# An mLSTM state update: three ScalarE copies and one GpSimd addition in place of three VectorE operations

## The chip, the core and the metric

The kernel runs on one core of one Trainium2 chip, as one launch. The core has five engines that run side by side, each through its own list of instructions, strictly in the order of that list: TensorE (PE, matmuls; PEld is its loading of weights), VectorE (DVE), ScalarE (ACT), GpSimd (POOL) and SyncE (SP, which here starts all DMAs). Where an instruction needs another engine's result it waits on a semaphore, and everything behind it on its own engine waits too. The metric is the device time of the launch in microseconds (us), lower is better. Before the change it is 406.48 us, the median of three runs (405.6 to 406.5).

## What is computed

Three layers one after the other, all in float32. The first is an mLSTM over 2 batches, 8 heads, 768 steps and heads of width 40. The changed line belongs to it:

```
for t in range(S):
    m_new = np.maximum(f_gate[t] + m, i_gate[t])
    f_stab = np.exp(f_gate[t] + m - m_new);  i_stab = np.exp(i_gate[t] - m_new);  m = m_new
    C = f_stab * C + i_stab * outer(v[t], k[t])        # state, 40 x 40 per head
    n = f_stab * n + i_stab * k[t]
    y[t] = sigmoid(o_gate[t]) * (C @ q[t]) / max(|n . q[t]|, 1)
```

The second layer takes x (1536 tokens x 320) to `max(x@w1, x@w2, x@w3) @ w_out` with an inner width of 768. The third takes that to `mish(z @ w_in) @ w_out2` with an inner width of 2048.

## The kernel before, in words

**The mLSTM in chunks.** The 768 steps are cut into six chunks of 128, so with two batches there are 12 units (u = 2 * chunk + batch). Unit u works on 128 steps of all eight heads of one batch at once. Its pieces, with the names that the rows use: `spread` broadcasts the forget gates with eight matmuls into two PSUM banks (fp, L139); `decay` turns each bank into decay factors with a VectorE scan (dt, L124); `scores` multiplies keys and queries into the same two banks (sc, L162), so the scores of a unit can't be written before both of its scans have read them; `decayed` multiplies scores and decays (dt, L167); `passed` and `queries` make the queries scaled by the decay since the chunk's start (cp on PE, cb on VectorE, L178); `values` and `keys` scale v and k on GpSimd (vp L173, kp L184). `numer` (it, L204 and L206) is the sum of two parts: the scaled queries times the state carried in (st), and the decayed scores times vp. `denom` and `gated` turn it into the unit's output (den, sg, xn), `transpose_x` brings that to the layout of the next layer (xp, xh) and `lower_x` makes its low part (xl).

**The state.** There is one tile st per batch, 120 x 8 x 41: three heads stacked on the partitions, a column block of 41 for each head, with zeros wherever a partition's head is not that column's. `outer` (sp, L256) multiplies kp and vp in three matmuls into one PSUM bank; its off-diagonal blocks are to be dropped. `carry` first multiplies st by the chunk's decay (three ScalarE instructions, L268), and then adds the wanted blocks of sp: three VectorE operations (L270), each for every third head, multiply sp by a mask column and add st. Units 2 to 9 do this, eight times in all (units 0 and 1 start the state with L264, units 10 and 11 need no state after them).

**The layers behind.** Float32 values are split into a high and a low part, and one product is eight matmuls of 512 columns (`mm8`, L339). `up(blk, m)` makes three such products (mm_m_0 to mm_m_2) for a block of 512 tokens, takes their maximum (ACT L354, DVE L356 twice) and splits it (ACT hh L358, POOL hl L359). The three products share three PSUM banks, so the product after next waits for the reading of the one before. Their weights arrive as raw bits and are decoded: dec (ACT L285), low (DVE L292, L294), dec (DVE L296), then split (ACT L307 to L309, POOL L310 to L312). There are nine such pieces w_0 to w_8, then three for `down` (wo; L330 to L332), later more for the third layer. Two buffers hold dec, so a piece is started when the split of the piece two before it is done.

**What sets the order.** The first third is written out by hand on all engines, up to unit 3 and the first up(0, 0). The rest is written as plans (PLAN0: `w` load weights, `u` up, `o` load wo, `a` attend, `b` finish of a unit), and a scheduler orders each engine's list from its own model of durations; it sets the lists when the kernel is built, and on the chip they are fixed. Units 0 to 3 are the tokens of block 0, units 4 to 7 those of block 1, and units 8 to 11 those of block 2, so the mLSTM of later units runs between the matmuls of earlier blocks.

Of the kernel before, what the change touches and what calls it, by code (L numbers as in the profile page):

```python
# [8 lines left out]
F32 = mybir.dt.float32  # L9
F32R = mybir.dt.float32r  # L10
AF = mybir.ActivationFunctionType
ALU = mybir.AluOpType
# [3 lines left out]
B, H, S, D = 2, 8, 768, 40  # L16
# [7 lines left out]
VD = D + 1  # L24
# [18 lines left out]
def mlstm_moe_kernel(ctx, tc, fi0, fir, qk2, q3, nat, w13, wo1, wi2, wo2, ident, bmask, out):  # L43
    nc = tc.nc
# [15 lines left out]
    a2 = at.enter_context(tc.tile_pool(name="a2", bufs=2))  # L60
# [12 lines left out]
    bmt = ac.tile([120, H], F32, tag="bmt", name="bmt")  # L73
# [8 lines left out]
    st = [ac.tile([120, H, VD], F32, tag=f"st{b}", name=f"st{b}") for b in range(B)]  # L82
# [177 lines left out]
    def carry(u):  # L260
        c, b = u // B, u % B
        sp = unit[u]["sp"]
        if c == 0:
            return nc.vector.tensor_tensor(st[b], sp[:, 0:H], bmt[:, 0:H].unsqueeze(2).to_broadcast([120, H, VD]), op=ALU.mult)  # L264
        dc = unit[u]["dc"]
        for g in range(3):
            h1 = min(3 * g + 3, H)
            nc.scalar.activation(st[b][:, 3 * g:h1], st[b][:, 3 * g:h1], AF.Copy, scale=dc[:, g])  # L268
        for j in range(3):
            nc.vector.scalar_tensor_tensor(st[b][:, j::3], sp[:, j:H:3], bmt[:, j:j + 1], st[b][:, j::3], op0=ALU.mult, op1=ALU.add)  # L270

    raws = {}

# [117 lines left out]
    with tc.manual_schedule(engines={ET.PE, ET.DVE, ET.SP, ET.Activation, ET.Pool}):  # L391
# [5 lines left out]
        f, i = ft0[:, 0], ft0[:, 1]  # L397
# [69 lines left out]
        nc.scalar.activation(sel40.rearrange("p (r d) -> p r d", d=D), idt[:, P + BH:P + 2 * BH + 1].unsqueeze(2).to_broadcast([P, BH + 1, D]), AF.Copy)  # L467
        denom(0)
        carry(0)
        nc.vector.tensor_tensor_scan(cpr, fr, z1r, 0.0, op0=ALU.mult, op1=ALU.add)  # L470
        nc.scalar.activation(fzr[64:64 + BH], cpr, AF.Copy)
# [13 lines left out]
        nc.scalar.activation(gTr, gq[:, 0:NR * BH], AF.Copy)  # L485
        denom(1)
        carry(1)
        decayed(2, 0)
        decayed(2, 1)
# [52 lines left out]
        fdve = lower_x(3)  # L542
        fpool = load_w13(1)
        carry(2)
        carry(3)
        up(0, 0, 0)
# [221 lines left out]
```

## Time and profile before

| what | before |
|---|---|
| median of 3 runs | 406.48 us (405.6 to 406.5) |
| profiled execution, its own time | 405.76 us |
| its span, first to last instruction | 403.9 us |
| busy share PE / PEld | 97% / 85% |
| busy share DVE / ACT / POOL | 54% / 43% / 39% |
| granted TensorE clock | 1.000 throughout |

The span is what the trace shows, the remaining 1.86 us lie around it. A matmul's end in the trace is modelled, so that two neighbours overlap; the distance between starts tells what one costs in a row of them. Busy shares over the whole span hide stages: up to about 95 us weights are decoded, and DVE, ACT and POOL are busy; behind it PE is busy nearly alone.

### The profile page before, as it was taken

To read this page: it belongs to the slowest core of one execution; us is meant where nothing else is said; L and a number is where in the kernel's file an instruction comes from. 1 tells how busy PE (TensorE), PEld (TensorE's weight loads), DVE (VectorE), ACT (ScalarE), POOL (GpSimd) and SP (SyncE) were. 2 spreads that over 40 slices of the span, in tenths; PEclk is the share of its full clock that TensorE was granted. 3 is DMA by queue.
4 is the path that set the end of the run, shared out by engine and by line. 5 is a ranking of instruction groups with operands and counts; after the bars stand their busy time and mean duration, and the time that the engine had idled before them with its cause. 6 is when DMAs were issued, how large, how long until landed. Compare 5 with 4: busy or idle time off the path is not lost.

```text
span 403.9 us, 6179 instructions
## 1 busy us (share of the span) xinstructions
PE 393.0 (97%) x2380; PEld 345.0 (85%) x2384; DVE 218.1 (54%) x342; ACT 172.4 (43%) x387; POOL 156.6 (39%) x155
## 2 busy tenths in 40 slices
PE   8999999879999999999999999999999999999996
PEld 4977887758898888888888899999898999999996
DVE  7988999998335577305922869972212221222220
ACT  3545655564143212246442586653332333434331
POOL 7556768995313223338851455661000010001000
PEclk9999999999999999999999999999999999999999
DMA  7786455636302011001420234300100000100001
GB/s 202 217 291 190 151 191 197 205 137 185 100 2 82 20 65 68 0 2 43 152 67 0 73 125 137 124 1 2 65 0 2 1 2 0 67 0 2 34 0 34
DMA packets 10410, 32.62 MB, mean 81 GB/s; under 512 B 1405, under 2 KB 4285, under 8 KB 10381
## 3 DMA queue, kind: packets, MB, share of 16 engines
q1 hardware_dynamic: 10381, 32.23, 24.9%
q8 instruction: 19, 0.31, 0.4%
q14 instruction: 10, 0.08, 0.1%
HBM read 30.26 MB, written 1.97 MB: 80 GB/s over the span
## 4 chain that ended last, share of the span: by engine, by line
PE 84%; DVE 8%; POOL 4%; issue 3%; ACT 1%; DVEq 0%; POOLq 0%
PE h L339 22%; PE mm L339 18%; PE o L662 7%; PE o L660 7%; PE o L661 7%; PE it L206 4%; PE mz L370 2%; PE mz L372 2%; PE mz L371 2%; PE fp L139 2%; PE sc L162 2%; DVE dt L124 2%; PE it L204 2%; PE wps L193 2%; PE sp L256 1%
## 5 line engine op out<-in xcount | busy, mean ns | idle before, releaser
L644 DVE TENSOR_TENSOR gl<-g,gh 128x512 fp32r<-128x512 f32 (+1 forms) x64 | 38.3, 599 | 97.3 <-ACT g L643 97.3
L339 PE MATMUL mm<-xh,w 128*128 128x512 f32 x270 | 73.1, 397 | 1.5 <-DVE zraw L356 0.9
L339 PE MATMUL h<-zh,wi 128*128 128x512 f32 (+1 forms) x320 | 67.7, 338 | 0.0
L642 ACT ACTIVATE gh<-h 128x512 fp32r<-128x512 f32 (+1 forms) x64 | 31.4, 491 | 83.6 <-PE h L339 77.6
L339 PEld LDWEIGHTS mm<-xh,w 128*128 128x128 f32 x270 | 49.4, 188 | 12.5 <-DVE zraw L356 1.0
L662 PE MATMUL o<-wo,gl 128*128 128x320 f32 x192 | 59.4, 309 | 0.0
L661 PE MATMUL o<-wo,gh 128*128 128x320 f32 x192 | 59.4, 309 | 0.0
L660 PE MATMUL o<-wo,gh 128*128 128x320 f32 x192 | 59.2, 309 | 0.0
L339 PEld LDWEIGHTS h<-zh,wi 128*128 128x128 f32 x320 | 51.4, 189 | 4.7
L613 POOL TENSOR_TENSOR zl<-zraw,zh 128x512 fp32r<-128x512 f32 (+1 forms) x12 | 13.0, 1091 | 91.5 <-ACT zh L612 91.5
L339 PE MATMUL mm<-xl,w 128*128 128x512 f32 x162 | 46.9, 393 | 0.0
L339 PE MATMUL h<-zl,wi 128*128 128x512 f32 (+1 forms) x192 | 44.5, 338 | 0.0
L359 POOL TENSOR_TENSOR hl<-zraw,hh 128x512 fp32r<-128x512 f32 x18 | 25.9, 1441 | 46.8 <-ACT hh L358 46.7
L356 DVE TENSOR_TENSOR zraw<-zraw,mm 128x512 f32<-128x512 f32 x36 | 24.5, 681 | 29.1 <-PE mm L339 29.0
L660 PEld LDWEIGHTS o<-wo,gh 128*128 128x128 f32 x192 | 36.1, 188 | 1.3
L661 PEld LDWEIGHTS o<-wo,gh 128*128 128x128 f32 x192 | 36.1, 188 | 1.2
L662 PEld LDWEIGHTS o<-wo,gl 128*128 128x128 f32 x192 | 36.1, 188 | 0.0
L339 PEld LDWEIGHTS mm<-xl,w 128*128 128x128 f32 x162 | 30.2, 188 | 6.4
L339 PEld LDWEIGHTS h<-zl,wi 128*128 128x128 f32 x192 | 31.8, 188 | 4.1
L643 ACT ACTIVATE g<-h 128x512 f32<-128x512 f32 (+1 forms) x64 | 31.2, 487 | 0.0
L124 DVE TENSOR_TENSOR_SCAN dt<-fp,idr 128x512 f32<-128x512 f32 x24 | 28.3, 1207 | 2.3 <-PE fp L139 2.2
L206 PE MATMUL it<-vp,dt 128*128 128x41 f32 x192 | 25.0, 271 | 0.0
(138 smaller groups left out, 630.7 us busy)
## 6 DMA issues: line engine op xcount, KB each, us to landing
raw_wo<-in_wo_dram SPq DMA_DIRECT2D x11, 640.0 KB
na<-in_nat_dram SPq DMA_DIRECT2D x12, 484.0 KB
raw_w<-in_w_dram SPq DMA_DIRECT2D x9, 640.0 KB
raw_wi<-in_wi_dram SPq DMA_DIRECT2D x8, 640.0 KB
qall<-in_qk_dram SPq DMA_DIRECT2D x24, 160.0 KB
out_dram<-ob SPq DMA_DIRECT2D x12, 160.0 KB
q<-in_q_dram SPq DMA_DIRECT2D x10, 180.0 KB
idt<-in_ident_dram SPq DMA_DIRECT2D x1, 80.5 KB
```

What stands on the lines that cost most here:

```text
L124: nc.vector.tensor_tensor_scan(dtf[:, j * 512:(j + 1) * 512], unit[u]["fp"][j], idr, 0.0, op0=ALU.mult, op1=ALU.add)
L206: nc.tensor.matmul(it[:, h], t["dt"][:, h], vt[:, h], start=(c == 0), stop=(c == 0 or h == h1 - 1))
L339: nc.tensor.matmul(ps, a, r, start=(k == 0), stop=(k == 7))
L356: tops[blk, m] = nc.vector.tensor_tensor(top, top, pss[i], op=ALU.max)
L359: nc.gpsimd.tensor_tensor(ls, top, h.bitcast(F32), op=ALU.subtract)
L613: nc.gpsimd.tensor_tensor(zl[:, j], zv[:, j], zh[:, j].bitcast(F32), op=ALU.subtract)
L642: mark[blk, m] = nc.scalar.activation(gh, ps, AF.Mish)
L643: nc.scalar.activation(g, ps, AF.Mish)
L644: low[blk, m] = nc.vector.tensor_tensor(gl, g, gh.bitcast(F32), op=ALU.subtract)
L660: nc.tensor.matmul(po, a, whi, start=(m == 0), stop=False)
L661: nc.tensor.matmul(po, a, wlo, start=False, stop=False)
L662: nc.tensor.matmul(po, l, whi, start=False, stop=(m == KF2 - 1))
```

## The change

After the scaling by the decay, the masked product is no longer added by VectorE. ScalarE copies the wanted blocks of sp out of PSUM, times the mask column, into a new SBUF tile nw (three copies, L271 in the new file), and one GpSimd addition adds nw to the whole state tile (L272). The tile nw has one buffer for all units.

```
         for g in range(3):
             h1 = min(3 * g + 3, H)
             nc.scalar.activation(st[b][:, 3 * g:h1], st[b][:, 3 * g:h1], AF.Copy, scale=dc[:, g])
+        nw = a2.tile([120, H, VD], F32, tag="nw", bufs=1, name=f"nw{u}")
         for j in range(3):
-            nc.vector.scalar_tensor_tensor(st[b][:, j::3], sp[:, j:H:3], bmt[:, j:j + 1], st[b][:, j::3], op0=ALU.mult, op1=ALU.add)
+            nc.scalar.activation(nw[:, j::3], sp[:, j:H:3], AF.Copy, scale=bmt[:, j:j + 1])
+        nc.gpsimd.tensor_tensor(st[b], st[b], nw, op=ALU.add)
```

Two lines are added, so from there on the new file's line numbers are higher by two (L285 becomes L287, L339 becomes L341). The scheduler orders the plans anew, and so instructions that the diff doesn't touch stand elsewhere too. Three places follow. In the names the first digits tell the unit, the block or the weight piece (st0 is batch 0, nw2 unit 2, w13_8 the piece w_8, mm0_5_1 the product 5_1 of block 0); the last number only tells tiles apart.

The first is ScalarE's list from the carries of units 2 and 3 on (39 us in the trace of before). Before:

```order
L268 ACTIVATE st0_98<-st0_98,dc2_352 120x123 x2
L268 ACTIVATE st0_98<-st0_98,dc2_352 120x82
L268 ACTIVATE st1_99<-st1_99,dc3_408 120x123 x2
L268 ACTIVATE st1_99<-st1_99,dc3_408 120x82
L285 ACTIVATE dec_w13_2_568<-raw_w13_2_511 128x640
L188 ACTIVATE sg4_626<-na4_583 128x320
L188 ACTIVATE sg5_718<-na5_675 128x320
L154 ACTIVATE dc4_618<-cp4_614 120x3
L354 ACTIVATE zraw_70<-mm0_0_0_533 128x512
```

The same place now:

```order
L268 ACTIVATE st0_98<-st0_98,dc2_352 120x82
L271 ACTIVATE nw2_524<-sp2_475,bmt_88 120x3x41 x2
L271 ACTIVATE nw2_524<-sp2_475,bmt_88 120x2x41
L268 ACTIVATE st1_99<-st1_99,dc3_408 120x123 x2
L268 ACTIVATE st1_99<-st1_99,dc3_408 120x82
L287 ACTIVATE dec_w13_2_572<-raw_w13_2_511 128x640
L188 ACTIVATE sg4_630<-na4_587 128x320
L188 ACTIVATE sg5_722<-na5_679 128x320
L154 ACTIVATE dc4_622<-cp4_618 120x3
L128 ACTIVATE dl4_606<-dt4_603 128x8
L287 ACTIVATE dec_w13_3_632<-raw_w13_3_493 128x640
L154 ACTIVATE dc5_714<-cp5_710 120x3
```

Three copies (nw2) now stand ahead of the decode of w_2, and the reading of the first product (mm0_0_0) has moved behind the decode of w_3 and behind the three copies nw3, which come next in the list.

The second is GpSimd's list at the split of w_8, around the carry of unit 4 (75 to 82 us). Before:

```order
L173 TENSOR_TENSOR vp0_91<-na6_841,gTr_101 128x328
L184 TENSOR_TENSOR kp0_89<-na6_841,dl6_860 128x320
L247 TENSOR_TENSOR xl1_582<-xr4_760,xh1_581 128x3x128
L310 TENSOR_TENSOR w13_8_909<-dec_w13_8_903,w13_8_909 128x512
L311 TENSOR_TENSOR w13_8_909<-dec_w13_8_903,w13_8_909 64x128
L312 TENSOR_TENSOR w13_8_909<-dec_w13_8_903,w13_8_909 64x128
L216 TENSOR_TENSOR sg5_718<-sg5_718,den5_815 128x320
```

And now:

```order
L173 TENSOR_TENSOR vp0_91<-na6_849,gTr_101 128x328
L184 TENSOR_TENSOR kp0_89<-na6_849,dl6_868 128x320
L247 TENSOR_TENSOR xl1_586<-xr4_764,xh1_585 128x3x128
L272 TENSOR_TENSOR st0_98<-st0_98,nw4_774 120x328
L312 TENSOR_TENSOR w13_8_917<-dec_w13_8_911,w13_8_917 128x512
L313 TENSOR_TENSOR w13_8_917<-dec_w13_8_911,w13_8_917 64x128
L314 TENSOR_TENSOR w13_8_917<-dec_w13_8_911,w13_8_917 64x128
L216 TENSOR_TENSOR sg5_722<-sg5_722,den5_821 128x320
```

The addition stands between unit 4's xl and the split of w_8, and the gating of unit 5 (sg5) comes behind both.

The third is TensorE's list from the scores of unit 7 to the numerator of unit 6 (87 to 92 us). Before:

```order
L162 MATMUL sc7_0_937<-qall_93 128x128 x4
L162 MATMUL sc7_1_938<-qall_93 128x128 x4
L150 MATMUL cp7_947<-fzr_97,sel40_96 120x128 x3
L339 MATMUL mm0_4_2_1092<-xh0_103,w13_7_894 128x512 x4
L339 MATMUL mm0_4_2_1092<-xl0_104,w13_7_894 128x512 x3
L339 MATMUL mm0_5_0_1182<-xh0_103,w13_7_894 128x512
L204 MATMUL it6_1018<-st0_98,cb6_881 128x123
```

And now, from the last scores on:

```order
L162 MATMUL sc7_0_945<-qall_93 128x128
L162 MATMUL sc7_1_946<-qall_93 128x128
L341 MATMUL mm0_5_0_1192<-xh0_103,w13_7_902 128x512
L150 MATMUL cp7_955<-fzr_97,sel40_96 120x128 x3
L341 MATMUL mm0_5_0_1192<-xh0_103,w13_7_902 128x512 x3
L341 MATMUL mm0_5_0_1192<-xl0_104,w13_7_902 128x512 x3
L341 MATMUL mm0_5_1_1193<-xh0_103,w13_8_917 128x512 x5
L341 MATMUL mm0_5_1_1193<-xl0_104,w13_8_917 128x512 x3
L204 MATMUL it6_1026<-st0_98,cb6_889 128x123
```

When the numerator of unit 6 is reached, the list of before has one matmul of product 5_0 behind it, and the new one all eight of 5_0 and all eight of 5_1: fifteen matmuls more. The other matmuls ahead of that point (the scores, the spreads and the rest of units 4 to 7) are the same ones.

## Rows read from the trace of the kernel before

**Rows 1.** The page's first part: busy us, share of the span, instructions.

```profile
PE 393.0 (97%) x2380; PEld 345.0 (85%) x2384; DVE 218.1 (54%) x342; ACT 172.4 (43%) x387; POOL 156.6 (39%) x155
```

**Rows 2.** Stretches: length, busy us of each engine, clock, DMA share, GB/s.

```profile
60.00:70.00 10.00, 9.10 (x55) 7.47 (x54) 9.97 (x15) 5.15 (x12) 8.96 (x9) 1.00 0.60 202
70.00:80.00 10.00, 9.27 (x58) 7.61 (x56) 9.01 (x16) 5.92 (x16) 8.85 (x9) 1.00 0.59 188
80.00:90.00 10.00, 6.86 (x44) 5.24 (x43) 9.39 (x13) 6.29 (x13) 9.25 (x9) 1.00 0.45 159
90.00:100.00 10.00, 9.69 (x59) 8.29 (x59) 8.78 (x16) 4.22 (x11) 6.12 (x7) 1.00 0.64 181
100.00:110.00 10.00, 10.00 (x60) 8.15 (x59) 3.29 (x8) 1.68 (x4) 3.68 (x4) 1.00 0.35 107
```

**Rows 3.** PE's groups, 40 to 95 us: busy, mean ns; idle before, releaser.

```profile
L162 PE MATMUL sc<-qall 64*128 64x128 f32 x64 | 8.5, 289 | 3.2 <-DVE dt L124 3.2
```

**Rows 4.** Lines L268 and L270: count, shortest/median/longest ns, first and last start.

```profile
L268 ACT ACTIVATE st<-st,dc x24: 346/384/399, 39.4 to 146.0; 120x123 f32<-120x123 f32 x16, 120x82 f32<-120x82 f32 x8
L270 DVE SCALAR_TENSOR_TENSOR st<-sp,bmt,st x24: 289/330/347, 41.5 to 155.8; 120x123 f32<-120x123 f32 x16, 120x82 f32<-120x82 f32 x8
```

**Rows 5.** Timeline, 39 to 43 us: start, length, engine, line, what, count.

```profile
39.40 1.77 ACT L268 ACTIVATE st<-st,dc 120x123 f32<-120x123 f32 x6
41.08 0.76 ACT L285 ACTIVATE dec_w<-raw_w 128x640 f32<-128x640 f32 x1
41.48 1.50 DVE L270 SCALAR_TENSOR_TENSOR st<-sp,bmt,st 120x123 f32<-120x123 f32 x6
41.61 1.43 POOL L173 TENSOR_TENSOR vp<-na,gTr 128x328 f32<-128x328 f32 x2
42.53 0.57 ACT L354 ACTIVATE zraw<-mm 128x512 f32<-128x512 f32 x1
42.90 0.82 DVE L294 SCALAR_TENSOR_TENSOR low_w<-dec_w,low_w 128x640 int32<-128x640 int32 x1
```

**Rows 6.** Timeline, 55 to 90 us: DVE beside POOL, and carries four and five.

```profile
55.02 0.81 DVE L296 SCALAR_TENSOR_TENSOR dec_w<-raw_w,low_w 128x640 int32<-128x640 int32 x1
72.71 0.80 DVE L270 SCALAR_TENSOR_TENSOR st<-sp,bmt,st 120x123 f32<-120x123 f32 x3
84.14 1.74 DVE L296 SCALAR_TENSOR_TENSOR dec_wo<-raw_wo,low_wo 128x640 int32<-128x640 int32 x1
85.15 1.85 POOL L359 TENSOR_TENSOR hl<-zraw,hh 128x512 fp32r<-128x512 f32 x1
88.89 1.31 POOL L173 TENSOR_TENSOR vp<-na,gTr 128x328 f32<-128x328 f32 x1
89.54 0.80 DVE L270 SCALAR_TENSOR_TENSOR st<-sp,bmt,st 120x123 f32<-120x123 f32 x3
```

**Rows 7.** Timeline, 77 to 83 us: POOL up to unit 5's gating.

```profile
77.06 1.60 POOL L247 TENSOR_TENSOR xl<-xr,xh 128x384 fp32r<-128x384 f32 x1
78.61 1.30 POOL L310 TENSOR_TENSOR w<-dec_w,w 128x512 fp32r<-128x512 f32 x1
81.51 0.85 POOL L216 TENSOR_TENSOR sg<-sg,den 128x320 f32<-128x320 f32 x1
82.40 0.49 DVE L221 TENSOR_TENSOR xn<-it,sg 128x320 f32<-128x320 f32 x1 [0.61 <-POOL sg L216]
```

**Rows 8.** Timeline, 85 to 93 us: PE's waits in brackets, and cb of unit 6.

```profile
87.06 1.16 PE L162 MATMUL sc<-qall 64*128 64x128 f32 x8 [1.39 <-DVE dt L124]
88.58 1.16 PE L162 MATMUL sc<-qall 64*128 64x128 f32 x8 [0.36 <-DVE dt L124]
91.80 0.54 DVE L178 TENSOR_TENSOR cb<-cp,q 120x384 f32<-120x384 f32 x1
92.39 0.48 PE L204 MATMUL it<-st,cb 120*128 120x123 f32 x2 [0.31 <-DVE cb L178]
```

**Rows 9.** The chain that ended last: start, length, what; matmuls behind unit 6's numerator.

```profile
95.96 4.84 PE mm L339 x21
```

## The prediction, written before the changed kernel ran

> **What bounds the kernel now.** I read the busy shares first [rows 1]: PE stands at 97%, the other three at about half. That alone would say that nothing on DVE matters. The stretches say otherwise [rows 2]. From 100 us on PE is full and DVE has a third of its time taken; but in the ten microseconds from 80 on PE is busy for only 6.86, and DVE for 9.39 and POOL for 9.25. The four stretches from 60 to 100 leave PE 0.90 + 0.73 + 3.14 + 0.31 = 5.08 us idle. This is the room that the change can work in; behind it, PE's own list is the time, and what DVE saves there costs and gives nothing. The groups of PE [rows 3] name the largest wait: 3.2 us ahead of the scores, whose two banks have to be read by DVE's scans first. The timeline [rows 8] shows it at work: the scores of unit 7 wait 1.39 and 0.36 us for scans that stand in DVE's queue, and the numerator of unit 6 waits 0.31 us for cb, also on DVE. So up to about 95 us the time is set by a chain that runs through DVE's queue and, at its side, POOL's.
>
> **What is removed.** 24 VectorE operations, 289 to 347 ns each [rows 4], eight groups of three. A group in a row takes 0.80 us [rows 6], so 6.4 us leave DVE in all. Only four groups lie ahead of 95 us: units 2 and 3 (1.50 us together [rows 5]) and units 4 and 5 (0.80 each [rows 6]). The other four lie in stretches where PE is full; they count for nothing.
>
> **What is added on ScalarE.** 24 copies. The trace of before has no such copy of 120 x 3 x 41 out of PSUM. From below, the scalings of the same size follow each other every 1.77 / 6 = 0.295 us [rows 5]; from above, one lasts up to 0.399 us alone [rows 4]. I take the lower, since they stand in a row: 0.89 us for a group, 1.2 at most. ACT is half idle [rows 2], so most of them are covered, with one exception. At the first two carries the list is full: the six scalings start at 39.40, and the decode of w_2 follows at 41.08 [rows 5]. Now three copies stand in front of it, so it ends near 42.73 in place of 41.84. DVE needs that decode for L294, which began at 42.90, when the six removed operations were just done. So DVE, 1.50 us earlier free, waits for ACT, and keeps 0.1 to 0.2 us of it. The six copies also push back the reading of the first product, from 42.53 by roughly 3 to 3.5 us (two groups of 0.89, and the decode and small copies that the new list puts ahead of it). Its bank is wanted again only by the fourth product, and the 16 matmuls of the second and third stand ahead of that, 3.7 us at 0.23 each [rows 9], so this is about covered. I book the first two carries at nothing. Uncovered, it would cost up to 1.8 us, the two groups.
>
> **What is added on GpSimd.** Eight additions of 120 x 328, also not in the trace. The nearest row is vp of 128 x 328: two of them in 1.43 us, 0.72 each [rows 5], and 1.31 us where DVE works beside it [rows 6]. I take 0.75 to 0.9. The first two stand behind two vp that end at 43.04 [rows 5] and ahead of the split of w_2, which has to wait for DVE's decoding of w_2 from 42.90 on in any case; the addition for unit 4 falls where POOL has no room. From xl at 77.06 over the split of w_8 to sg at 81.51 its operations touch each other, and DVE's xn of unit 5 waits 0.61 us for the end of it [rows 7]. The addition goes between, and I count 0.8 us of delay for w_8, for sg and for the decode buffer behind it. The one for unit 5 stands behind xl of that unit near 90 us, ahead of operations that only later matmuls need.
>
> **DVE and POOL against each other.** The final decoding operation lasts 0.81 us at 55.02 and 1.74 at 84.14, where POOL's operation at 85.15 lies beside it [rows 6]; the removed L270 never moves outside 289 to 347 ns [rows 4]. So what is removed is of a kind that was not disturbed, and what is added on POOL may disturb others: by up to 0.93 us each, twice in the full stretch, and not at all if the scans or the readings of products happen to run beside it. I take 0.4 each, the middle. The Trainium skill ("SBUF — State Buffer", section "SBUF: two separate sides") says that a VectorE operation with two SBUF inputs and a GpSimd one take a shared port in turn, whole instructions at a time; the longer row at 84.14 agrees. By it alone each addition could cost DVE its full length, and the full stretch would give up twice 0.75 where I count twice 0.4: 0.7 us more, 403.9 in place of 403.2.
>
> Sum on DVE and POOL up to cb of unit 6: saved 2 x 0.80 = 1.6; lost 0.8 (addition ahead of w_8) + 0.8 (disturbance) + about 0.5 (small waits, an allowance like the 0.61 and 0.31 that rows 7 and 8 show). That is 0.5 us later: cb of unit 6 starts near 92.3 in place of 91.80, and the numerator near 92.9 in place of 92.39 [rows 8].
>
> **What is moved on TensorE, the larger term.** The new list reaches that numerator with fifteen 512-column matmuls more behind it. In the row of 21 that followed the numerator's stretch before, one costs 4.84 / 21 = 0.23 us [rows 9], so 3.45 us of work are taken out of the stretch behind 95 us, which PE bounds, and put into the idle 5.08 us [rows 2]. They have to fit there. Product 5_1 needs w_8, split by 82.3 in my count; 5_0 needs the bank that ACT frees; both are asked for after the scores at about 89. It fits, if the scans come no later than before. Behind the numerator, the cover stays what it was: between the spread of unit 8 and its first scores stand 21 matmuls in either list, 7 + 8 + 6 before, 8 of product 5_2 and 13 of `down` now. So the lead isn't used up by the next wait of the same kind. SyncE's list starts a few loads of later units earlier, one of them ahead of w_8's; the DMA engines are 0.45 to 0.64 busy there [rows 2], and I book nothing for it.
>
> Sum: -3.45 + 0.5 = -2.95 us. Against the profiled execution's own 405.76 this gives 402.8. That execution is at the lower end of the three runs; against the median of 406.48 it gives 403.5. I say 403.2, between the two.
>
> **The rivals.**
>
> *No change: the lead is paid back.* The attention chain, not PE's work, is the clock up to 95 us, and the extra matmuls only stand in front of things that then come later. For it: DVE at 9.97 of 10 and POOL near 9 of 10 from 60 to 70 [rows 2] have no slack, and the additions take POOL's. Against it: the waits of PE [rows 8] are real idle time, and 15 matmuls fill it wherever DVE is. It needs the numerator of unit 6 some 2.3 to 4.6 us later than 92.39: the lost 0.8, the full 1.86 of disturbance and the 1.8 of the first carries uncovered, less 1.6, make 2.9. Time 405.2, within a band of 404.6 to 407.0. The skill's "Perfetto Trace Analysis", section "Optimizing Scalar/DVE Operations", warns that moving work from VectorE to GpSimd may not help; the row at 84.14 speaks for that warning, the low busy shares of the stretch from 100 us on against it.
>
> *Slower: ScalarE's queue holds up the weights.* One buffer holds nw, so the copies for unit 3 wait for the GpSimd addition of unit 2, which waits behind two vp (until 43.04 [rows 5]). Behind these copies stand the reading of the first product and the split of w_2, and then every weight piece in turn, since two decode buffers tie each piece to the one before. If this shift of 1.8 to 2.7 us goes through the chain whole, and the additions cost 1.31 each for units 4 and 5, with 1.86 of disturbance, the numerator comes 1.8 to 2.7 + 2.6 + 1.9 - 1.6 = 4.7 to 5.6 us late, less the 3.45: 1.3 to 2.1 slower, about 407.5. It decides from a numerator that starts later than 97.0 (92.39 + 3.45 + 1.2).
>
> *Faster by more.* POOL's additions hide, no disturbance, and DVE's 1.6 us reach the numerator: -3.45 - 1.6 = -5.05, all the idle there is: 400.7.
>
> **How the numbers follow.** 0.3% of 406.48 is 1.2 us, about what a measurement can tell from no change. Chances: the forecast (with -1.3 to -4.2 around it) 0.50, the faster one 0.12, no change 0.22, slower 0.16. So faster 0.62, same 0.22, slower 0.16. The likeliest case alone gives 402.0 to 405.0. For eight in ten I go from 401.0 up to 407.2: below, about half of the faster case is left out; above, the worse half of the slower one.
>
> **What would show it.** Right: PE's idle time from 60 to 100 us falls from 5.1 us to about 2; unit 6's numerator starts between 91.5 and 94 with product 5_1 done; from there to the end the span is as long as before less 3.45 us; a copy lasts 0.3 to 0.4 us, an addition 0.7 to 0.9; the decode of w_2 on ACT is about 0.9 us later and DVE idles ahead of L294. Wrong: PE waits for a weight split or a product's bank in the first stretch (45 to 60 us); the numerator after 95; new waits for st or for ScalarE behind 100 us; or a scan that comes 2 us later because of the split of w_8.

## The result and the profile after: slower by 0.7%

The changed kernel takes 409.31 us, the median of four runs (408.38 to 409.78), against 406.44 us for the kernel before beside it. The ratio is 1.0073 with an interval of 1.0054 to 1.0093: slower, where 403.2 was forecast. The profiled execution took 408.38 us, the least of the four; its span is 406.5 us.

The page's first part, where [rows 1] stand for before: VectorE gave up 5.2 us, ScalarE took on 6.9 and GpSimd 7.1. TensorE's busy time rose by 1.7 us, although its list holds the same work.

```profile
PE 394.7 (97%) x2384; PEld 345.8 (85%) x2384; DVE 212.9 (52%) x318; ACT 179.3 (44%) x411; POOL 163.7 (40%) x163
```

The stretches that answer to [rows 2], then the ten microseconds around 92 us in pieces of two (columns as in [rows 2]; the clock is the seventh figure, the one before the DMA share).

```profile
60.00:70.00 10.00, 9.50 (x53) 7.37 (x52) 9.97 (x15) 5.86 (x14) 7.44 (x8) 1.00 0.51 176
70.00:80.00 10.00, 9.13 (x59) 7.61 (x59) 8.61 (x14) 6.79 (x18) 8.43 (x8) 1.00 0.51 161
80.00:90.00 10.00, 5.17 (x29) 3.80 (x30) 8.28 (x8) 4.68 (x8) 8.24 (x10) 0.98 0.38 132
90.00:100.00 10.00, 10.00 (x50) 8.50 (x50) 7.03 (x11) 5.95 (x15) 8.35 (x8) 0.68 0.63 213
...
88.00:90.00 2.00, 0.56 (x3) 0.56 (x4) 2.00 (x3) 0.74 (x1) 0.90 (x2) 0.88 0.27 64
90.00:92.00 2.00, 2.00 (x13) 1.77 (x13) 2.00 (x4) 1.46 (x4) 2.00 (x3) 0.50 0.67 264
92.00:94.00 2.00, 2.00 (x8) 1.67 (x8) 1.90 (x3) 1.24 (x6) 2.00 (x2) 0.50 0.00 0
94.00:96.00 2.00, 2.00 (x6) 1.52 (x6) 2.00 (x5) 1.07 (x3) 2.00 (x4) 0.50 0.58 136
96.00:98.00 2.00, 2.00 (x10) 1.59 (x9) 0.44 (x1) 1.38 (x2) 2.00 (x2) 0.91 0.99 399
```

Two things are new. TensorE is busy for 5.17 of the ten microseconds from 80 on, where it was 6.86. And right behind that its clock is granted at half (1.2 in place of 2.4 GHz): the last 0.48 us ahead of 90, six whole microseconds, and 0.36 us behind 96, 6.84 us in all. PE reads as 10.00 there because every matmul lasts twice as long; the x50 beside it is what tells. At half speed 6.84 us do the work of 3.42.

TensorE's timeline shows the place (start, length, operation, in brackets the wait ahead; it answers to [rows 8]).

```profile
84.80 0.53 PE L233 MATMUL xp<-idt,xn 128*128 128x128 f32 x3 [1.21 <-DVE xn L221]
86.34 0.40 PE L341 MATMUL mm<-xh,w 128*128 128x512 f32 x1
89.44 3.19 PE L162 MATMUL sc<-qall 64*128 64x128 f32 x16 [2.70 <-DVE dt L124]
...
98.20 0.38 PE L204 MATMUL it<-st,cb 120*128 120x123 f32 x2
```

The scores of unit 7 wait 2.70 us in one piece for their scans; before they waited 1.39 and 0.36. Unit 6's numerator starts at 98.20 in place of 92.39. What GpSimd did ahead of it (the rows answer to [rows 7]):

```profile
79.42 0.88 POOL L272 TENSOR_TENSOR st<-st,nw 120x328 f32<-120x328 f32 x1
80.26 1.85 POOL L312 TENSOR_TENSOR w<-dec_w,w 128x512 fp32r<-128x512 f32 x1
...
83.40 0.72 POOL L216 TENSOR_TENSOR sg<-sg,den 128x320 f32<-128x320 f32 x1
...
84.50 1.27 POOL L334 TENSOR_TENSOR wo<-dec_wo,wo 128x512 fp32r<-128x512 f32 x1
85.72 1.85 POOL L361 TENSOR_TENSOR hl<-zraw,hh 128x512 fp32r<-128x512 f32 x1
```

VectorE's rows in the same stretch (they answer to xn5 in [rows 7] and to what released the scores in [rows 8]):

```profile
84.16 0.49 DVE L221 TENSOR_TENSOR xn<-it,sg 128x320 f32<-128x320 f32 x1 [1.69 <-POOL sg L216]
84.56 1.88 DVE L296 SCALAR_TENSOR_TENSOR low_wo<-dec_wo,low_wo 128x640 int32<-128x640 int32 x1
86.48 1.77 DVE L298 SCALAR_TENSOR_TENSOR dec_wo<-raw_wo,low_wo 128x640 int32<-128x640 int32 x1
88.18 2.32 DVE L124 TENSOR_TENSOR_SCAN dt<-fp,idr 128x512 f32<-128x512 f32 x2
```

The addition for unit 4 stands ahead of the split of w_8, and sg5 starts at 83.40 (before 81.51; e2 and e7 below tell what of this is the addition's). VectorE, which the change relieved, idles 1.69 us for it (before 0.61). Then come the two last decoding operations of wo_1. They stood ahead of unit 7's scans before, too, with a maximum between them, but there the first of them took 0.81 us; now it takes 1.88. VectorE's rows of before, then GpSimd's beside the second of them:

```profile
82.81 0.81 DVE L294 SCALAR_TENSOR_TENSOR low_wo<-dec_wo,low_wo 128x640 int32<-128x640 int32 x1
85.80 1.21 DVE L124 TENSOR_TENSOR_SCAN dt<-fp,idr 128x512 f32<-128x512 f32 x1
```

```profile
83.90 1.29 POOL L332 TENSOR_TENSOR wo<-dec_wo,wo 128x512 fp32r<-128x512 f32 x1
```

How long they last can be read off GpSimd's rows. L334 ends at 84.50 + 1.27 = 85.77, and low_wo ends at 86.44, 0.67 later; L361 ends at 87.57, and dec_wo at 88.25, 0.68 later. The same operation undisturbed takes 0.81 us [rows 6]. So VectorE's operation did its work when GpSimd's was over, and not beside it. The Trainium skill says why ("SBUF — State Buffer", section "SBUF: two separate sides"): the port pair that the two share is a lock, whichever starts first has it for a whole instruction. The rows agree: in the twelve traces there are 400 rows of one such operation (128x640, two SBUF inputs) that lasted over 0.85 us, and every one of them ends 0.67 to 0.70 us behind the end of a GpSimd operation that began before it or with it; the other 272 took 0.79 to 0.84.

### The profile page after: what moved, and what is told of

Its sections match the earlier page's. It is cut to its first block, busy times and chain, and to the rows that moved or that the text cites. A ratio compares the mean times of both kernels' runs of the same rounds, so it can differ in the third digit from the quotient of the medians.

```text
span 406.5 us, 6195 instructions
## 1 busy us (share of the span) xinstructions
PE 394.7 (97%) x2384; PEld 345.8 (85%) x2384; DVE 212.9 (52%) x318; ACT 179.3 (44%) x411; POOL 163.7 (40%) x163
## 4 chain that ended last, share of the span: by engine, by line
PE 82%; POOL 6%; DVE 5%; ACT 3%; issue 2%; POOLq 0%; DVEq 0%; ACTq 0%
PE h L341 21%; PE mm L341 17%; PE o L664 7%; PE o L662 7%; PE o L663 7%; PE it L206 4%; PE sc L162 3%; PE fp L139 2%; PE mz L372 2%; PE mz L373 2%; PE mz L374 2%; PE it L204 2%; PE wps L193 1%; POOL w L312 1%; DVE dec_w L298 1%
## 5 line engine op out<-in xcount | busy, mean ns | idle before, releaser
L341 PE MATMUL mm<-xh,w 128*128 128x512 f32 x270 | 74.4, 403 | 2.1 <-DVE zraw L358 0.9
L341 PE MATMUL h<-zh,wi 128*128 128x512 f32 (+1 forms) x320 | 67.4, 338 | 0.0
L341 PEld LDWEIGHTS mm<-xh,w 128*128 128x128 f32 x270 | 49.8, 191 | 14.0 <-ACT zraw L356 1.4
L341 PEld LDWEIGHTS h<-zh,wi 128*128 128x128 f32 x320 | 51.4, 189 | 4.8
L341 PE MATMUL mm<-xl,w 128*128 128x512 f32 x162 | 47.3, 397 | 0.0
L341 PE MATMUL h<-zl,wi 128*128 128x512 f32 (+1 forms) x192 | 44.6, 338 | 0.0
L361 POOL TENSOR_TENSOR hl<-zraw,hh 128x512 fp32r<-128x512 f32 x18 | 25.5, 1418 | 43.9 <-ACT hh L360 43.8
L341 PEld LDWEIGHTS mm<-xl,w 128*128 128x128 f32 x162 | 30.7, 191 | 6.5
L341 PEld LDWEIGHTS h<-zl,wi 128*128 128x128 f32 x192 | 31.8, 188 | 4.1
```

Source lines behind the costliest of these rows:

```text
L341: nc.tensor.matmul(ps, a, r, start=(k == 0), stop=(k == 7))
L361: nc.gpsimd.tensor_tensor(ls, top, h.bitcast(F32), op=ALU.subtract)
```

## The experiments

Beside each other, every kernel with a trace. "sg4 to xn5" is from the start of unit 4's gating on GpSimd to that of unit 5's xn on VectorE; a difference between two starts leaves out what lies ahead of both. The last column is the span less the numerator's start. The medians come from several chips, each with the kernel before beside it (medians of 406.2 to 406.4); the ratios compare with that.

| kernel | median us | sg4 to xn5 | xn5 to scores of 7 | scores to numerator of 6 | numerator at | rest |
|---|---|---|---|---|---|---|
| before | 406.4 | 16.67 | 4.66 | 5.33 | 92.39 | 311.5 |
| after | 409.31 | 18.08 | 5.28 | 8.76 | 98.20 | 308.3 |
| e1 new operations, old order | 409.89 | 17.62 | 4.66 | 7.69 | 96.90 | 311.7 |
| e2 old operations, new order | 407.34 | 17.09 | 5.32 | 9.23 | 97.99 | 308.3 |
| e3 wait filled | 405.98 | 18.07 | 5.29 | 6.07 | 95.78 | 308.3 |
| e4 scans first | 405.90 | 18.07 | 2.51 | 8.78 | 96.33 | 308.4 |
| e6 moves together | 402.11 | 17.10 | 4.05 | 4.98 | 92.35 | 308.4 |
| e7 addition behind sg5 | 403.67 | 17.11 | 4.06 | 5.96 | 93.23 | 308.4 |
| e8 units 2, 3 as before | 409.33 | 18.07 | 5.29 | 8.84 | 98.61 | 308.3 |
| e10 moves, old operations | 402.74 | 17.10 | 4.08 | 4.96 | 92.65 | 308.4 |
| e11 spare addition ahead | 407.11 | 17.45 | 4.80 | 5.17 | 93.34 | 311.5 |
| e12 spare addition behind | 406.49 | 16.67 | 4.77 | 7.70 | 95.81 | 311.5 |

The rest is 311.5 to 311.7 with the old order of TensorE and 308.3 to 308.4 with the new one, whatever happened ahead. So the lead is real, 3.2 us of the 3.45 forecast, and all else is decided before the numerator.

What lies ahead of sg4 can be told apart, too. Whole executions lie up to 1.3 us apart already at VectorE's scans ahead of the first carries (here before, then after; 40.16 in e12):

```profile
39.23 2.33 DVE L124 TENSOR_TENSOR_SCAN dt<-fp,idr 128x512 f32<-128x512 f32 x2
38.89 2.33 DVE L124 TENSOR_TENSOR_SCAN dt<-fp,idr 128x512 f32<-128x512 f32 x2
```

From there to sg4 it is 26.50 us in before and 26.51 in e11 and e12, which have its lists. In the new order it is 27.41 to 27.44 where units 2 and 3 are carried as before (e2, e8, e10) and 27.17 to 27.20 where they are carried as changed (after, e3, e4, e6, e7). In e1, the old order with the changed carries, it is 27.65. So the new order costs 0.9 us ahead of sg4, the changed carries win back 0.25 of that in it, and cost 1.15 in the old order.

In the experiments all five lists are held in a given order, so nothing is re-planned by accident; their line numbers are a few higher for that.

**e1 and e2: arithmetic and order apart.**

```
 e1: the lists of before      e2: the lists of after
-VectorE: st += sp * mask    -ScalarE: nw = sp * mask;  GpSimd: st += nw
+ScalarE: nw = sp * mask     +VectorE: st += sp * mask
+GpSimd:  st += nw
```

> The changed arithmetic (copies on ScalarE, addition on GpSimd), with all five lists held in the order of the kernel before; only the new copies and additions are placed between them. Theory A (the order is what costs: unit 7's scans behind a decode, TensorE idle in one piece, then the clock at half for 6.83 us, 3.4 us in all): the scans of unit 7 start at 86 to 88 as before, no wait ahead of its scores is longer than about 1.8 us, the clock stays at 1.00, and what is left is the price of the operations themselves, 0 to 1.5 us: 405.5 to 407.5. Theory B (the operations cost: GpSimd's additions and what they hold up on VectorE): the time stays with the changed kernel's, 408.5 to 409.8, with a wait over 2 us ahead of the scores of unit 7 in the old order too.

> The arithmetic of before (three VectorE operations), with all five lists held in the order of the changed kernel. Theory A: the two scans of unit 7 still stand behind the decode of wo_1, so TensorE waits about 2 to 2.7 us ahead of the scores of unit 7; if the clock falls to half behind that as in the changed kernel, 407.5 to 409.5; if it does not fall, the lead of 15 matmuls is kept and the time is 402.5 to 404.5. Theory B: without the additions the time goes back to that of before, 405.8 to 406.8, wherever the scans stand.

> The arithmetic of before with the lists of the changed kernel, once more, for a trace (the profiled execution of the first run of it was 937 us long and shows nothing). Theory E: without the addition ahead of w_8 sg5 starts near 82.5 in place of 83.4, the scans of unit 7 well before 88.18, and TensorE's wait ahead of its scores is under 1.5 us although the scans stand behind the decode of wo_1; 405.3 to 407.8. Rival A (the order alone makes the long wait): the wait is 2.4 us or longer.

e1: 409.89, ratio 1.0061 (1.0033 to 1.0090); four of its twelve executions took 407.0 to 408.0, the other eight 409.7 to 410.7, the profiled one 410.4. Theory A falls as it was put: the old order didn't save the time. But B's long wait isn't there either, the scores wait as long as in before (TensorE's timeline of e1):

```profile
89.21 1.16 PE L163 MATMUL sc<-qall 64*128 64x128 f32 x8 [1.39 <-DVE dt L125]
90.73 2.07 PE L163 MATMUL sc<-qall 64*128 64x128 f32 x8 [0.36 <-DVE dt L125]
```

The second row's matmuls last twice as long: the clock fell to half here too, behind the same two waits that left it at 1.00 in the profiled execution of before. Three parts make the 4.51 us to the numerator. 1.20 us lie ahead of sg4, and 1.15 of them behind the scans at 39 us, where the first carries are what differs: three copies (nw) wait 1.18 us for GpSimd's addition, and the reading of the first product behind them starts at 45.27 in place of 42.53 (ScalarE's timeline of e1).

```profile
44.55 0.84 ACT L272 ACTIVATE nw<-sp,bmt 120x123 f32<-120x123 f32 x3 [1.18 <-POOL st L274]
45.27 0.61 ACT L359 ACTIVATE zraw<-mm 128x512 f32<-128x512 f32 x1
```

0.95 us are the addition ahead of w_8 (17.62 against 16.67), and 2.36 us the clock (7.69 against 5.33).

e2: 407.34, ratio 1.0005 (0.9981 to 1.0029), between what theories A (from 407.5) and B (up to 406.8) said; three of its executions took 405.4 to 405.5 us, eight 407.1 to 407.7, and one 937.82. The trace is that of a further execution, which took 408.12 with a mean clock of 0.987 (0.995 or 0.996 in those eleven), so it shows more of the clock's loss than they had. In it the wait at the scores is 1.17 us, under the 1.5 that E allowed, but TensorE came late to it, behind 3.4 us at half clock, and 408.12 is above E's 407.8. sg5 starts at 82.56, as E said, and relative to sg4 xn5 comes 0.99 us earlier than in after. But the decoding ahead of the scans stays long, and the clock fell twice (its mean is 0.89 from 80 to 84, 0.68 in the four microseconds behind and 0.50 from 92 to 96). TensorE's wait, then VectorE's rows ahead of it, from that trace:

```profile
88.76 0.71 PE L163 MATMUL sc<-qall 64*128 64x128 f32 x4 [1.17 <-DVE dt L125]
```

```profile
83.85 1.91 DVE L296 SCALAR_TENSOR_TENSOR low_wo<-dec_wo,low_wo 128x640 int32<-128x640 int32 x1
85.79 1.78 DVE L298 SCALAR_TENSOR_TENSOR dec_wo<-raw_wo,low_wo 128x640 int32<-128x640 int32 x1
87.49 2.32 DVE L125 TENSOR_TENSOR_SCAN dt<-fp,idr 128x512 f32<-128x512 f32 x2
```

So the new order alone costs 0.9 us ahead of sg4, 0.42 up to xn5 (17.09 against 16.67) and 0.66 from there to the scores, and takes back 3.2 at the end; with the old arithmetic the two about cancel once the clock's loss is in.

**e3: fill the wait.**

```
+        for _ in range(11):      # into the bank of cp6, between sp5 and cp6
+            nc.tensor.matmul(full, fill[:, 0:P], fill[:, 0:512], start=True, stop=True)
```

> The changed kernel with its own lists, plus eleven matmuls of 128x512 without use on TensorE, where it would wait ahead of the scores of unit 7 (2.70 us in the changed kernel; eleven at 0.23 are 2.5 us). Theory A: TensorE is busy in place of waiting, the clock stays at 1.00 through 89 to 97 us, the numerator of unit 6 starts near 95 in place of 98.20, and the kernel is 3 to 3.4 us faster than the changed one: 405.7 to 406.5. Rival C (the halved clock only lies beside a stretch that VectorE's queue bounds, so it costs little): the clock stays up but the time does not, 408.3 to 409.6.

405.98, ratio 0.9980 (0.9960 to 1.0000), 3.33 us less than after, by adding work. The clock is 1.00 in all of its twelve executions. TensorE's timeline of e3, the added matmuls first (one of the eleven has no record):

```profile
86.27 2.32 PE L155 MATMUL cp<-idr 128*128 128x512 bf16 x10
...
89.71 0.71 PE L172 MATMUL sc<-qall 64*128 64x128 f32 x4 [0.33 <-DVE dt L126]
90.82 1.16 PE L172 MATMUL sc<-qall 64*128 64x128 f32 x12 [0.41 <-DVE dt L126]
...
95.78 0.38 PE L214 MATMUL it<-st,cb 120*128 120x123 f32 x2
```

VectorE and GpSimd are as late as in after (18.07 and 5.29 in the table), so rival C is out: the halved clock itself costs the time, 3.33 us between the medians and 2.4 between the two profiled executions (408.38 and 406.00). From the scores to the numerator e3 takes 6.07 us where after takes 8.76, so 2.69 us of that stretch are the clock's. The other 0.74 over before's 5.33 are TensorE's own: the new list has fifteen 512-column matmuls there, the old one eight, and behind 90.82 nothing is waited for.

**e4: the scans first.**

```
 VectorE  xn5
+         scans of unit 7 (two)
          low, dec of wo_1
-         scans of unit 7 (two)
```

> The changed kernel with its own lists but one move on VectorE: unit 7's two scans stand right behind xn of unit 5, ahead of the two last decoding operations of wo_1 (1.88 and 1.77 us there) in place of behind them. Theory A: the scans end near 87 in place of 90.5, the wait of 2.70 us ahead of the scores of unit 7 falls below 1 us, the clock stays at 1.00; the numerator of unit 6 then waits for its scaled queries, which stay at about 94.3, and starts at 94.6 to 95.3 in place of 98.20: 405.5 to 406.5. Theory B: the additions still delay all else, 408.3 to 409.6.

405.90, ratio 0.9978 (0.9957 to 0.9998). The wait at the scores is gone, but the gain is not whole (TensorE's timeline of e4):

```profile
87.55 1.43 PE L163 MATMUL sc<-qall 64*128 64x128 f32 x16
...
91.12 0.53 PE L151 MATMUL cp<-fzr,sel 128*120 128x128 f32 x3 [1.70 <-ACT xr L247]
...
96.33 0.38 PE L205 MATMUL it<-st,cb 120*128 120x123 f32 x2
```

The next wait in line had stood covered: ScalarE reads unit 5's transposed output only behind the split of wo_1. The clock fell behind it again, for 3.4 us (its mean is 0.83 from 90 to 100). The two executions in which it stayed at 1.00 took 404.37 and 404.39, but one with a mean clock of 0.996 took 404.37 as well. The time lies where it was expected; the clock, which was to stay at 1.00, does not.

**e7: one addition, four places further back.**

```
 GpSimd  xl4
-        st += nw   (unit 4)
         split of w_8 (three)
         sg5
+        st += nw   (unit 4)
```

> The changed kernel with its own lists but one move on GpSimd: the addition for unit 4 stands behind sg5 in place of ahead of the split of w_8. Theory D: w_8's split, sg5, xn5 and with it the scans of unit 7 start about 0.9 us earlier; TensorE's wait ahead of the transposes of unit 5 falls from 1.21 to 0.3 us, the one of about 2.7 us ahead of the scores stays, since the decode of wo_1 still stands ahead of the scans. If the clock still falls behind it the time is 408.0 to 408.8, if it does not, 404.5 to 405.5. Rival (the additions cost by sharing with VectorE, not by their place): within 0.4 us of the changed kernel, and sg5 no earlier.

403.67, ratio 0.9918 (0.9886 to 0.9951): 5.6 us faster than after, and below the 404.5 that I had as the best case. Relative to sg4, sg5 comes 1.10 us and xn5 0.97 us earlier, as expected. But the scans come 2.55 us earlier, not 0.9, and the long wait at the scores, which was to stay, is gone. GpSimd's rows of e7 from sg5 on:

```profile
82.32 0.85 POOL L217 TENSOR_TENSOR sg<-sg,den 128x320 f32<-128x320 f32 x1
83.14 0.89 POOL L273 TENSOR_TENSOR st<-st,nw 120x328 f32<-120x328 f32 x1
83.98 1.04 POOL L334 TENSOR_TENSOR wo<-dec_wo,wo 128x128 fp32r<-128x128 f32 x1
84.98 1.85 POOL L335 TENSOR_TENSOR wo<-dec_wo,wo 128x512 fp32r<-128x512 f32 x1
```

VectorE's rows of e7 behind sg5:

```profile
83.61 1.09 DVE L297 SCALAR_TENSOR_TENSOR low_wo<-dec_wo,low_wo 128x640 int32<-128x640 int32 x1
84.74 0.97 DVE L299 SCALAR_TENSOR_TENSOR dec_wo<-raw_wo,low_wo 128x640 int32<-128x640 int32 x1
85.63 2.33 DVE L125 TENSOR_TENSOR_SCAN dt<-fp,idr 128x512 f32<-128x512 f32 x2
```

The decoding operations now end 0.67 us after the addition (84.03) and 0.69 after the short L334 (85.02): they wait for short neighbours, and the long L335 is the one that waits, 1.85 in place of 1.27. Together 2.06 us in place of 3.65. The scores of unit 7 start at 87.27 with no wait ahead that the timeline shows, and the numerator at 93.23. The clock still fell (its mean is 0.83 from 80 to 90, and 0.50 from 84 to 86), but ahead of the scores, and it cost nothing there: the three executions at 1.00 throughout (404.15, 404.20, 404.48) are no faster than the other five (403.50 to 403.67).

**e8: units 2 and 3 as before.**

```
+        if u < 4:   # three VectorE operations, as before
+            return
         nw = a2.tile(...)
```

> The changed kernel with its own lists, but the carries of units 2 and 3 done by the three VectorE operations each as before; the six other carries stay on ScalarE and GpSimd. Theory D, first part (the six copies and two additions at 39 to 45 us make the first weights late, and this lateness of about 0.8 us goes through to unit 5): sg5 and xn5 start 0.6 to 0.9 us earlier; with the clock still halved behind the wait at unit 7's scores 408.0 to 408.8, without that 404.5 to 405.5. Rival (the first carries are covered, as I had booked them): the time within 0.4 us of the changed kernel's, 408.9 to 409.6, and sg5 where it was.

409.33, ratio 1.0055 (1.0030 to 1.0080): the rival holds. In the new order the changed first carries cost nothing (sg4 even comes 0.25 us earlier with them); the 18.07 from sg4 to xn5 is that of after.

**e6 and e10: the moves together, with either arithmetic.**

```
 GpSimd   st += nw (unit 4) behind sg5; vp6 ahead of the split of wo_1
 VectorE  scans of 7, cb6, one maximum ahead of low, dec of wo_1
 ScalarE  xh5, xr5, dc6 ahead of the split of wo_1
 e10: the same lists, VectorE's three operations in place of copies and addition
```

> The changed arithmetic in the changed kernel's lists, with these moves between 80 and 95 us: on GpSimd the addition for unit 4 behind the gating of unit 5 (sg5), and vp of unit 6 ahead of the split of wo_1; on VectorE unit 7's two scans, cb of unit 6 and one maximum ahead of the last two decoding operations of wo_1; on ScalarE the copies of unit 5's transposed output ahead of the split of wo_1. Theory D (the delays before about 90 us add up, and the waits they leave end in the halved clock): sg5 and xn5 about 0.9 us earlier than with the additions ahead of them, no wait over 1 us at the scores of unit 7 or behind them, the clock at 1.00, the numerator of unit 6 at 93 to 94, and a time of 402.8 to 404.2. Rival (TensorE's own list or another chain, as the bare arithmetic change, sets the time): no better than the kernel with the scans first, 405 to 406.5.

> The same lists as in the kernel with the moves together, but the arithmetic of before: three VectorE operations for each carry, no ScalarE copies and no GpSimd additions. Theory D: the operations themselves then matter little either way, with 1.6 us more on VectorE and 1.7 us less on GpSimd between 70 and 95 us: within 1 us of the kernel with the moves together, 402.3 to 404.5, and below before's by over 1 us. Rival (the changed arithmetic is what costs, in any order): clearly faster than the kernel with the moves together, by 1.5 us or more. Third way (VectorE's queue is the bound, and the change of arithmetic is a gain once the order allows it): slower than it by 1 us or more.

e6 is at 402.11, ratio 0.9867 (0.9831 to 0.9903), faster than both kernels: 7.2 us below after, and below the 402.8 that I had as the best case. e10 is at 402.74 (0.9883, 0.9847 to 0.9918). What theory D said of e10 holds: in these lists the arithmetic matters little either way. The medians lie 0.63 us apart. In the traces e10's numerator comes 0.26 us later than e6's, counted from the scans at 39 us, and all of that arises ahead of sg4; from sg4 on the two agree to 0.03 us in every column, although e10 has six VectorE operations there that e6 has not. Against the expectation the clock fell in both (mean 0.83 from 80 to 90). TensorE has no wait from the scores of unit 7 to the numerator (its timeline of e6):

```profile
87.37 1.17 PE L163 MATMUL sc<-qall 64*128 64x128 f32 x16
...
92.35 0.38 PE L205 MATMUL it<-st,cb 120*128 120x123 f32 x2
```

**e11 and e12: the addition alone, in the kernel before.**

```
 GpSimd  xl4
+        spare = idr + idr   (e11, 120x328, not used)
         split of w_8 (three)
         sg5
+        spare = idr + idr   (e12)
```

> The kernel before, its arithmetic and all its lists unchanged, plus one GpSimd addition of 120x328 without use, put between xl of unit 4 and the split of w_8, where the changed kernel has the addition for unit 4. Theory E (this one place carries the loss: sg5, xn5 and the scans of unit 7 come later by the addition and by what then lies beside VectorE's decoding, and TensorE's wait at the scores grows): sg5 starts 0.8 to 1.0 us later than in before, unit 7's first scores 0.9 to 2.5 us later, and the time is 407.0 to 409.5, the upper end if the clock falls to half behind the wait. Rival (what costs is the new order or the copies on ScalarE): 405.8 to 406.6, as before.

> The same addition without use in the kernel before, but behind sg5. Theory E: sg5, xn5 and the scans start where they did, within 0.3 us, and the time is that of before within 0.5 us, 405.8 to 406.9. Rival (an addition on GpSimd costs its 0.9 us or more wherever it stands near 80 us): as with the addition ahead of w_8, within 0.5 us of it.

e11 is at 407.11, ratio 1.0024 (0.9995 to 1.0052), e12 at 406.49, 1.0006 (0.9983 to 1.0028). The direction is E's, at its lower edge, and the interval of e11 just reaches no change. The trace is clearer than the times: from sg4 to xn5 17.45 and 16.67, so 0.78 us for an addition of 0.73 ahead of w_8 and nothing behind sg5. In e11 the scores of unit 7 come 0.92 us later relative to sg4, at the lower edge, too. GpSimd's rows of e11:

```profile
78.79 0.73 POOL L269 TENSOR_TENSOR spare<-idr 120x328 f32<-120x328 f32 x1
...
82.61 0.72 POOL L217 TENSOR_TENSOR sg<-sg,den 128x320 f32<-128x320 f32 x1
```

And e12's:

```profile
82.45 0.86 POOL L217 TENSOR_TENSOR sg<-sg,den 128x320 f32<-128x320 f32 x1
83.27 0.73 POOL L269 TENSOR_TENSOR spare<-idr 120x328 f32<-120x328 f32 x1
```

The rows of e12 lie 0.94 us later than in before throughout, because that execution began so. To read it one more thing is needed: in its profiled execution the clock fell to half behind the scores (7.70 from there to the numerator), with waits of 1.50 and 0.34 us; in five of its twelve executions, as in the profiled one of before, the clock was 1.00 throughout.

## Why the prediction was wrong

**What held.** A copy lasts 0.36 us and an addition 0.88, inside the 0.3 to 0.4 and 0.7 to 0.9 that were forecast (count, shortest, median, longest ns):

```profile
L271 ACT ACTIVATE nw<-sp,bmt x24: 319/358/383, 39.9 to 157.9; 120x123 f32<-120x123 f32 x16, 120x82 f32<-120x82 f32 x8
...
L272 POOL TENSOR_TENSOR st<-st,nw x8: 875/884/1476, 42.7 to 159.0; 120x328 f32<-120x328 f32 x8
```

The first carries, booked at nothing, cost nothing (e8), although in after VectorE idles 1.03 us ahead of L296, not 0.1 to 0.2. The fifteen matmuls were done ahead of the numerator, and the rest of the span is 3.2 us shorter. The addition ahead of w_8, booked at 0.8 us, cost 0.99 in the new order and 0.78 in the old one (e2, e11). Behind 100 us the other four carries cost nothing. So the larger term, -3.45, came as the sum had it, to a quarter of a microsecond. The prediction's own signs of failure came too: the numerator after 95, a scan over 2 us later behind the split of w_8, and TensorE's idle time from 60 to 100 us at 0.50 + 0.87 + 4.83 = 6.20 us, where it was to fall from 5.1 to about 2.

**The step that failed** is the sum on VectorE and GpSimd up to cb of unit 6, "saved 2 x 0.80 = 1.6; lost 0.8 + 0.8 + about 0.5", which put the numerator 0.5 us late. It came 5.81 us late, and 6.15 counted from the scans at 39 us, since the profiled execution of after began 0.34 us earlier. Four things were wrong in it:

- The 1.6 saved on VectorE was booked on the path. It isn't there: up to xn5 the path runs through GpSimd (sg5), and VectorE spends what it saved waiting (1.69 us for sg in place of 0.61). e6 and e10 show it directly for their lists: six VectorE operations less are worth nothing from sg4 to the numerator. The prediction's first paragraph says of the stretch behind 100 us that what VectorE saves gives nothing there; the same question was not asked of this stretch, where the row to ask it of was shown, the 0.61 that xn5 waits for sg [rows 7].
- The new order itself costs 0.69 us ahead of sg4 (0.9 less what the changed carries win back) and 0.42 from there to xn5, where the sum had 0.5 for small waits. The scores of unit 7 come 2.72 us later than in before, counted from the scans: these 1.11, the 0.99 of the addition, and 0.62 for the decoding ahead of the scans.
- The disturbance of VectorE by GpSimd was taken at 0.4 for each addition, a middle. It has no middle: an operation of VectorE with two SBUF inputs ends 0.67 to 0.70 us after the GpSimd operation that began before it. The price depends on the neighbour's length, and so on the order of both lists; e7 shows the same two operations at 2.06 and 3.65 us. That the 0.62 of the decoding lies near the 0.8 that was booked is luck. The row in [rows 6] was read wrongly, too: dec_wo at 84.14 ends at 85.88, 0.69 us behind the split at 83.90 (until 85.19), and the operation at 85.15, which the prediction names, is the one that waited. The Trainium skill's rule (the page and section named above) was priced in the prediction for the additions alone, at 0.7 us; it speaks of every such pair of the two engines.
- That TensorE's clock can fall was not in the sum at all, nor among the rivals, since the profile of before has 1.00 throughout. From the scores of unit 7 to the numerator it takes 3.43 us more than before (8.76 against 5.33): 2.69 are the clock's and 0.74 are what seven matmuls more take beyond the waits that they fill. They "have to fit" in the prediction, and where the scans come late they don't (e3). Between the medians of after and e3 the fall makes 3.33 us, more than the whole difference between before and after.

Together 0.69 + 0.42 + 0.99 + 0.62 + 0.74 + 2.69 = 6.15 us; less the lead of 3.2 that is 2.95, and the medians lie 2.87 apart. Without the clock the change would be at about 0.3, which is the rival "the lead is paid back". e3 sits there: its span is 404.1 us against 403.9 in before, and its median 405.98.

The fall was not new with the change. Of 77 executions of before that ran beside the experiments, 47 have a mean clock below 1.00. Most of them took no longer for it (405.4 to 406.7 us), but 14 took 408.9 to 409.2, as long as after, and one 411.6. In after all four executions have 0.992, and in e8 all twelve 0.987 or 0.992, at 408.4 to 410.4 us. So the change turned a loss that before has now and then into a regular one, and the one profile of before didn't show it.

**The slower rival** had the right sign and the wrong place: ScalarE's queue at the first carries. In after the copies for unit 3 wait 0.34 us for the addition, not 1.18 as in e1, because the new list puts the decode of w_3 ahead of them.

**What stays open.** Why the clock falls in one execution and not in another isn't settled. In before's order it stayed at 1.00 in the profiled execution behind waits of 1.39 and 0.36 us, and fell behind the same waits in e1. Filling the wait at the scores kept it at 1.00 (e3); taking that wait away by the order only moved the fall, behind the next wait in e4 and ahead of the scores in e6 and e7. No run set a wait's length alone. Where the new order loses its 0.9 us ahead of sg4 isn't taken apart, nor that the moves of e6 are worth 1.6 us over e7.

## What to carry to other kernels

Work taken from an engine counts only where that engine is what the next step waits for; ask first which engine's instruction releases it, and what the added work stands ahead of in that engine's queue. When operations move between VectorE and GpSimd, list the pairs that will lie side by side and take the later one as waiting for the earlier. And when a change lengthens a wait of TensorE, price the clock behind it too: useless matmuls in that wait won back 3.3 us, and moving a single addition behind the operation that others wait for won 5.6. One profiled execution doesn't tell whether the clock is safe: the kernel before lost about 3 us to it in 14 of 77.

## What the runs showed of the hardware that was not expected

TensorE's granted clock fell to half for 6.84 us behind waits of 0.87, 0.92, 1.21 and 2.70 us within eleven microseconds, and for 3.4 us at a time in e1 (0.83 mean from 70 to 80), e4, e6 and e7. What it costs depends on the place. In e7, where it fell ahead of the scores, it cost nothing; in e6 the three executions at 1.00 took 401.5 to 401.8 us and the other three 402.5 to 402.6, so about 1 us; in after it cost 2.4 to 3.3. In the trace the loss doesn't look like idleness: PE stands at 10.00 of 10.
